# A load whose 16 queues read neighbouring rows: the order of the attention input in memory

## The chip, the cores and the metric

The kernel runs on one core of one Trainium2 chip. The core has a matrix engine (TensorE, in the profile PE for its matmuls and PEld for its weight loads), a vector engine (VectorE, DVE), a scalar engine (ScalarE, ACT), a general engine (GpSimd, POOL) and an engine that only issues transfers and waits (SyncE, SP). Each takes its instructions in order, and they meet through semaphores. Data lies in the chip's memory, in the on-chip memory SBUF with its 128 partitions, and in PSUM, where matmuls put their results. Transfers between memory and SBUF are done by 16 DMA engines, which serve the queues of SP, ACT and POOL; one issued transfer is shared out over them.

The metric is the device time of one execution in microseconds (us). Lower is better.

## The reference

Two stages. The first is a causal attention without softmax, in which older positions fade (a retention), for 8 sequences of 576 positions, 8 heads of 64 (rel is the position of the row less that of the column):

```python
scores = scale * np.matmul(q, k.transpose(0, 1, 3, 2))
gamma = 1.0 - 2.0 ** (-5.0 - np.arange(H, dtype=np.float32))
Dmat = np.where(rel >= 0, gamma[:, None, None] ** rel[None, :, :], 0.0)
ret = scores * Dmat[None, :, :, :]
return np.matmul(ret, v).astype(np.float32)
```

Its result, as 4608 tokens of 512 numbers, goes through a mixture of 8 experts, of which each token takes one or none (probs is the softmax of the logits, mask picks the tokens of expert e):

```python
do_compute = x @ w_skip > 0
xc = x[do_compute]
logits = xc @ w_gate
e_idx = np.argmax(logits, axis=1)
gate_w = probs[np.arange(len(xc)), e_idx]
for e in range(E):
    h = np.maximum(xc[mask] @ w1[e], 0.0)
    y[mask] = gate_w[mask, None] * (h @ w2[e])
out[do_compute] = xc + y
```

## The kernel before

**Attention.** The work is cut into 36 groups g of 128 tokens (two sequences of one pair, 64 positions each; nine groups in a row make a pair's 576 positions). A group has one tile u of 128 partitions by 4 slots by 512 numbers, 1 MB. The host has put queries, keys and values into the array qkv in the very order in which u wants them, so that a group is loaded by two transfers of 512 KB: load_half (L433 to L446) with s = 0 fills the slots 0 and 1 (queries and keys, for the scores), with s = 2 the slots 2 and 3 (values and keys, for the running state). Each transfer gives every partition one piece of 4 KB.

For each group, TensorE makes the scores (L476, 64x64 blocks), the update of the running state (L528), the values (L556), and turns the result back to rows (L578). VectorE multiplies by the decay tables (decay, L494; xt, L567). POOL scales the keys for the state (keys, L514, tile kn), out of the second half of u. ACT copies the state out of PSUM into the next group's u (L539) and the finished rows to xn (L580), which ACT's own queue stores to out (L581, 256 KB).

**The order of the loads.** TensorE's order is the program's order (L661). Five buffers of u exist (UBUFS), and loads run up to four groups ahead (UAHEAD). Before the loop, the loads of the groups 0 to 3 are issued one after the other (L455 to L460). Within the loop over g, the second half of group g+3 is issued after the first block of products of group g, on which it is made to wait (L697, last_product), and the first half of group g+4 after the values of group g-1, whose buffer it takes over (L707). All of them stand on SP's queue. From group 32 on nothing is left to load.

**Routing.** Beside the attention, the logits of finished tokens are made (logits_a, logits_b), and VectorE gives each token its place with its expert (route_a, route_b, slots). The expert with the most tokens among the first ones is begun early (choose_first, close_first); its first five weight pieces (load_w, L130, 512 KB each, also on SP's queue) are loaded among the last loads of u.

**Experts.** From about 182 us on, the eight experts follow in order of size. Each has eight pieces of weights, loaded by SP, split into a high and a low part by ACT (L139) and VectorE (L140), and multiplied three times for accuracy (L387). Tokens are gathered (L303) and put back (L836) by indirect transfers that POOL issues.

The load that the change touches is in L437 and L438, both sides 128 x 1024, and the host's side of it in L1037:

```python
u_t[g][:, s : s + 2].rearrange("p s c a i -> p (s c a i)"),
qkv[g, s // 2],
...
qkv = qkv.reshape(NT, 2, P, 2 * DM)
```

Row p of qkv[g, h] goes to partition p, and the 128 rows of a load lie one after the other in memory, 512 KB in one piece.

Of the kernel before, what the change touches and what calls it, by code (L numbers as in the profile page):

```python
# [22 lines left out]
NTOK, DM, NE, DF = B * S, H * D, 8, 1024  # L23
P = 128
NT = NTOK // P
# [2 lines left out]
NCC = DM // P  # L28
NFC = DF // P
NBLK = 3  # L30

CAPS = (368, 344, 332, 308, 304, 286, 278, 276)
CAP = CAPS[0]
# [23 lines left out]
def kernel(  # L57
# [36 lines left out]
    make_identity(nc, ident)  # L94
    iota = const.tile([P, NBLK * P], F16, tag="iota", name="iota")
    nc.gpsimd.iota(iota, pattern=[[1, NBLK * P]], base=0, channel_multiplier=0, allow_small_or_imprecise_dtypes=True)
    desc = const.tile([P, NE], F32, tag="desc", name="desc")
# [79 lines left out]
    def route_b(ps, first, late, pin, n, t0, ex, mb, cb):  # L177
        c0 = NE * NCMP * NBLK + t0 * NE
        pr = ps[:, c0 : c0 + n * NE]
# [44 lines left out]

    def slot_match(t, nb=NBLK):

        r = rs_t[t] = rt.tile([P, NBLK * P], BF16, tag="r", name=f"r_{t}", bufs=NR)
        nc.vector.tensor_scalar(r[:, : nb * P], iota[:, : nb * P], trank[:, t : t + 1], None, ALU.is_equal)  # L228

    def slot_add(ps, t, first, last, nb=NBLK):  # L230
        r = rs_t.pop(t)
        for k in range(nb):
            nc.tensor.matmul(
                ps[:, k * NE * NCMP : (k + 1) * NE * NCMP],
                r[:, k * P : (k + 1) * P],
                mc[:, t, :],
                start=first and k == 0,
                stop=last,
                skip_group_check=True,
            )  # L240
# [174 lines left out]
    with ExitStack() as actx:  # L415
# [17 lines left out]
        def load_half(g, s, after=None):  # L433
            if s == 0:
                u_t[g] = ap.tile([P, 4, 2, NPR, D], F32, tag="u", name=f"u_{g}", bufs=UBUFS)
            half = nc.sync.dma_start(
                u_t[g][:, s : s + 2].rearrange("p s c a i -> p (s c a i)"),  # L437
                qkv[g, s // 2],  # L438
            )
            if after is not None:  # L440
                tc.add_manual_dep(
                    half.ins,
                    after.name,
                    mybir.DependencyInfo(mybir.DependencyClass.Sync, mybir.DependencyReason.DATA),
                    reason="the second half begins behind a block of products",
                )  # L446

        def load_u(g):
            for s in (0, 2):
                load_half(g, s)  # L450
# [241 lines left out]
        for g in range(NT):  # L692
            ahead = g + 1 < NT
            for c in range(2):
                in_turn(state(g, c), *([scores(g + 1, c)] if ahead else []))
                if c == 0 and g and g + UAHEAD - 1 < NT:
                    load_half(g + UAHEAD - 1, 2, last_product())  # L697
# [8 lines left out]
            if g + UAHEAD < NT:  # L706
                load_half(g + UAHEAD, 0)  # L707
# [15 lines left out]
        g = NT  # L723
# [332 lines left out]
```

## Time and profile before

| | |
|---|---|
| median of 3 executions | 429.39 us |
| lowest and highest | 425.88 and 430.9 us |
| the profiled execution | 428.38 us |
| its span, first to last instruction | 426.6 us |
| mean granted TensorE clock | 0.971 |

The profile is of one execution. Its page gives the busy time of each engine, the span in 40 equal slices of 10.7 us (a digit is the busy share in tenths), the DMA queues, the chain of work that ended last, the costliest groups of instructions, and the DMA issues with their median time from issue to landing. An entry such as "L514 POOL ... kn<-u" is line 514 of the kernel, run on POOL, writing kn from u. In the lists of waits, "A <- B: us, times, longest" says how long A's engine stood idle until B released it. DMA share is the mean busy share of the 16 DMA engines, GB/s is what they moved. The queue q1 is SP's, q10 is ACT's, q0 POOL's.

### The profile page before, as it was taken

The page shows a single profiled execution, that of the slowest core. Times are in us where ns is not written, and L with a number is a line of the kernel's source. Part 1 is how long each engine was busy: PE and PEld are TensorE (multiplying, and loading weights), DVE is VectorE, ACT ScalarE, POOL GpSimd, SP SyncE. Part 2 cuts the span into 40 slices and gives each one's busy share as a digit, 9 for nine tenths or more (in the row PEclk, how much of TensorE's full clock was granted, in tenths as well). Part 3 has the DMA queues.
Part 4 walks back from the last instruction along what each step waited for, and adds up shares of the span by engine and source line. Part 5 has one row for each costly group of instructions (what it writes and reads, how often), then busy time and mean ns, then how long its engine had stood idle before and what let it go on. Part 6 is the DMA issues. An engine that isn't in the chain of part 4 may idle for free.

```text
span 426.6 us, 13158 instructions
## 1 busy us (share of the span) xinstructions
PE 383.3 (90%) x5482; PEld 349.2 (82%) x5484; DVE 272.9 (64%) x570; ACT 176.1 (41%) x296; POOL 148.9 (35%) x166
## 2 busy tenths in 40 slices
PE   7888777978796878999999999999999999999990
PEld 3676666866675756888999999999999999999980
DVE  2567694688579888948745565775665665656430
ACT  1334343354344446216444434444534445455210
POOL 5833643364365468060150043032042151400302
PEclk9989998999999889999999999999999999999996
DMA  8889997999989985363765456456456466652101
GB/s 305 310 290 339 311 325 249 328 334 305 311 296 349 338 315 163 103 220 117 267 201 181 148 171 211 149 189 205 163 177 221 154 222 204 199 157 89 52 2 53
DMA packets 29135, 93.05 MB, mean 218 GB/s; under 512 B 3960, under 2 KB 4344, under 8 KB 29072
## 3 DMA queue, kind: packets, MB, share of 16 engines
q1 hardware_dynamic: 19584, 71.31, 50.2%
q0 software_dynamic: 3728, 11.04, 7.6%
q10 hardware_dynamic: 5760, 9.82, 6.1%
q8 instruction: 44, 0.72, 0.7%
q14 instruction: 19, 0.16, 0.1%
HBM read 77.98 MB, written 14.55 MB: 217 GB/s over the span
## 4 chain that ended last, share of the span: by engine, by line
PE 44%; DMA 22%; issue 16%; DVE 10%; POOL 4%; ACT 1%; another core or an unknown queue 1%; POOLq 0%; ACTq 0%; SPq 0%
DMA out<-rs,sidx 15%; PE py L387 10%; PE ph L387 9%; PE pxt L556 7%; PE ps_s L528 5%; PE px L578 4%; DMA xg<-out,gidx 3%; PE psc L476 3%; DVE u L494 2%; POOL out L836 2%; DVE r L228 2%; PE pl L586 2%; DMA out<-xn 1%; DMA u<-qkv 1%; POOL xg L303 1%
## 5 line engine op out<-in xcount | busy, mean ns | idle before, releaser
L140 DVE TENSOR_TENSOR wlo_w<-w,whi_w 128x1024 fp32r<-128x1024 f32 x59 | 71.9, 1223 | 56.5 <-ACT whi_w L139 56.4
L514 POOL TENSOR_TENSOR kn<-u,tt_sb 64x512 f32<-64x512 f32 x64 | 67.5, 1054 | 74.3 <-DMA u<-qkv 51.5
L836 POOL DMA_INDIRECT out<-rs,sidx x24 | 32.7, 1363 | 151.0 <-DVE rs L835 147.7
L139 ACT CAST whi_w<-w 128x1024 fp32r<-128x1024 f32 x59 | 61.6, 1051 | 57.5 <-PE py L387 53.9
L387 PE MATMUL py<-hhi,whi_w 128*128 128x344 f32 (+6 forms) x224 | 70.2, 313 | 0.0
L494 DVE TENSOR_TENSOR u<-psc,dt_sb 64x512 f32<-64x512 f32 x72 | 49.6, 689 | 30.9 <-PE psc L476 15.7
L387 PE MATMUL ph<-xhi,whi_w 128*128 128x344 f32 (+6 forms) x224 | 68.9, 307 | 0.0
L387 PE MATMUL py<-hhi,wlo_w 128*128 128x344 f32 (+6 forms) x224 | 67.7, 302 | 0.0
L387 PE MATMUL ph<-xhi,wlo_w 128*128 128x344 f32 (+6 forms) x224 | 67.7, 302 | 0.0
L387 PE MATMUL ph<-xlo,whi_w 128*128 128x344 f32 (+6 forms) x224 | 67.7, 302 | 0.0
L387 PE MATMUL py<-hlo,whi_w 128*128 128x344 f32 (+6 forms) x224 | 67.5, 302 | 0.0
L539 ACT COPY u<-ps_s 64x512 f32<-64x512 f32 x64 | 37.1, 579 | 46.7 <-PE psc L476 18.3
L528 PEld LDWEIGHTS ps_s<-u,kn 64*64 64x64 f32 x1024 | 36.9, 142 | 21.5 <-issue 13.1
L476 PE MATMUL psc<-u 64*64 64x64 f32 x1152 | 47.8, 230 | 7.0 <-issue 6.9
L556 PE MATMUL pxt<-u 128*64 128x64 f32 x1152 | 46.0, 233 | 8.3 <-issue 8.3
L395 ACT ACTIVATE hhi<-ph 128x344 fp32r<-128x344 f32 (+8 forms) x61 | 26.0, 426 | 64.3 <-PE ph L387 62.1
L528 PE MATMUL ps_s<-u,kn 64*64 64x64 f32 x1024 | 43.2, 231 | 9.9 <-issue 8.4
L556 PEld LDWEIGHTS pxt<-u 128*64 128x64 f32 x1152 | 39.9, 145 | 13.6 <-issue 11.3
L476 PEld LDWEIGHTS psc<-u 64*64 64x64 f32 x1152 | 41.0, 141 | 8.1 <-issue 7.7
L387 PEld LDWEIGHTS ph<-xhi,whi_w 128*128 128x128 f32 x224 | 42.3, 189 | 0.1
L387 PEld LDWEIGHTS ph<-xlo,whi_w 128*128 128x128 f32 x224 | 42.3, 189 | 0.1
L387 PEld LDWEIGHTS py<-hlo,whi_w 128*128 128x128 f32 x224 | 42.3, 189 | 0.0
(178 smaller groups left out, 641.3 us busy)
## 6 DMA issues: line engine op xcount, KB each, us to landing
u<-qkv SPq DMA_DIRECT2D x72, 512.0 KB, 5.8
w<-w SPq DMA_DIRECT2D x64, 512.0 KB, 3.6
out<-xn ACTq DMA_DIRECT2D x36, 256.0 KB, 5.9
out<-rs,sidx POOLq DMA_INDIRECT x24
xg<-out,gidx POOLq DMA_INDIRECT x21
dt_sb<-dtab ACTq DMA_DIRECT2D x1, 128.0 KB
gt_sb<-dtab ACTq DMA_DIRECT2D x1, 128.0 KB
wg_sb<-wg ACTq DMA_DIRECT2D x1, 64.0 KB, 8.3
```

Source lines behind the costliest of these rows:

```text
L139: nc.scalar.copy(hi, t)
L140: nc.vector.tensor_tensor(lo, t, hi.bitcast(F32), ALU.subtract)
L387: nc.tensor.matmul(ps, x, y, start=first and n == 0, stop=last and n == 3 * len(terms) - 1)
L395: nc.scalar.activation(hi, ph, AF.Relu)
L476: nc.tensor.matmul(psc_t[g][halves[j], c, a, :], u[halves[j], 1 - j, c, a, :], u[halves[j], j, c, a, :], start=c == 0 and a == 0, stop=c = ...
L494: nc.vector.tensor_tensor(u_t[g][h, j], psc[halves[j]], tab, ALU.mult)
L514: nc.gpsimd.tensor_tensor(kn_t[g][h], u_t[g][h, 2 + j], tab, ALU.mult)
L528: nc.tensor.matmul(ps_s[halves[j], c, a, :], kn_t[g][h, c, a, :], u_t[g][h, 3 - j, c, a, :], start=n == 0 and c == 0 and a == 0, stop=c == ...
L539: nc.scalar.copy(u_t[g + 1][halves[j], 3 - j], ps_s[halves[j]])
L556: nc.tensor.matmul(pxt[halves[j], a, c * D : (c + 1) * D], u_t[g][:, 3 - j, c, a, :], u_t[g][:, j, c, a, :], start=c == 0 and a == 0, stop ...
L578: nc.tensor.transpose(px[:, c * P : (c + 1) * P], xt_t[b][:, c, o * P : (o + 1) * P], ident)
L836: put = nc.gpsimd.indirect_dma_start(out=out, out_offset=bass.IndirectOffsetOnAxis(ap=sidx[:n, k, e : e + 1], axis=0), in_=rs[:n], in_offs ...
```

## The change

The host writes the 128 rows of a load in another order, and the load reads them back in the old one. Row p goes to the same partition p as before, and no other line is touched.

```diff
+NQUEUE = 16
...
             half = nc.sync.dma_start(
                 u_t[g][:, s : s + 2].rearrange("p s c a i -> p (s c a i)"),
-                qkv[g, s // 2],
+                qkv[g, s // 2].rearrange("r e x -> e r x"),
             )
...
+    def by_row(x):
+
+        x = x.reshape(*x.shape[:2], NQUEUE, P // NQUEUE, x.shape[-1])
+        return np.ascontiguousarray(x.transpose(0, 1, 3, 2, 4))
+
...
-    qkv = qkv.reshape(NT, 2, P, 2 * DM)
+    qkv = by_row(qkv.reshape(NT, 2, P, 2 * DM))
```

With p = 8 e + r, e from 0 to 15 and r from 0 to 7, row p lay at place 8 e + r of the load's 512 KB; now it lies at place 16 r + e. The array qkv has the shape 36 x 2 x 8 x 16 x 1024 in place of 36 x 2 x 128 x 1024. The source of a load is described by 16 entries (4 KB apart) of 8 rows (64 KB apart) of 4 KB, in place of 128 rows of 4 KB. The tile's side of the load is described as before, by 128 partitions of 4 KB. In the words of the change, e is the queue and r the row of that queue.

## The prediction

> **What bounds the kernel now.** I read the page first (shares, slices, queues), then the busy time by stage, then the waits, and last the loads' own landing times.
>
> ```profile
> span 426.6 us, 13158 instructions
> ...
> PE 383.3 (90%) x5482; PEld 349.2 (82%) x5484; DVE 272.9 (64%) x570; ACT 176.1 (41%) x296; POOL 148.9 (35%) x166
> ...
> DMA  8889997999989985363765456456456466652101
> GB/s 305 310 290 339 311 325 249 328 334 305 311 296 349 338 315 163 103 220 117 267 201 181 148 171 211 149 189 205 163 177 221 154 222 204 199 157 89 52 2 53
> ...
> q1 hardware_dynamic: 19584, 71.31, 50.2%
> q0 software_dynamic: 3728, 11.04, 7.6%
> q10 hardware_dynamic: 5760, 9.82, 6.1%
> ...
> u<-qkv SPq DMA_DIRECT2D x72, 512.0 KB, 5.8
> w<-w SPq DMA_DIRECT2D x64, 512.0 KB, 3.6
> out<-xn ACTq DMA_DIRECT2D x36, 256.0 KB, 5.9
> ```
>
> The span has two halves. In the first 15 slices (about 160 us) the DMA engines are eight to nine tenths busy at some 310 GB/s; after that they are at half. Only the first half issues the loads that the change touches: 72 loads of 512 KB into u, 37.7 MB. The 64 loads of w have the same size and keep their layout; they are the control. The same queue, q1, carries both.
>
> Busy time by stage; the columns are named in the second line:
>
> ```profile
> core 0 of [0], span 426.6 us
> core 0: us, PE busy (x) PEld busy (x) DVE busy (x) ACT busy (x) POOL busy (x), PEclk, DMA share, GB/s
> 0.00:3.00 3.00, 1.72 (x5) 0.62 (x6) 0.29 (x3) 1.25 (x1) 2.34 (x24) 1.00 0.31 70
> 3.00:14.00 11.00, 8.94 (x136) 5.28 (x139) 4.07 (x6) 1.39 (x4) 6.34 (x11) 0.84 1.04 401
> 14.00:150.00 136.00, 111.92 (x3271) 93.17 (x3262) 100.31 (x225) 57.31 (x100) 65.93 (x68) 0.96 0.91 312
> 150.00:182.00 32.00, 28.18 (x436) 22.43 (x433) 28.14 (x101) 14.48 (x25) 15.92 (x22) 0.95 0.56 193
> 182.00:300.00 118.00, 117.07 (x775) 113.07 (x774) 73.47 (x139) 51.60 (x85) 30.93 (x25) 1.00 0.57 187
> 300.00:410.00 110.00, 110.00 (x846) 109.76 (x846) 63.27 (x93) 48.92 (x80) 24.55 (x18) 1.00 0.49 156
> ```
>
> From 182 us on PE is busy for 227 of 228 us: that half is PE's, and no load of u is in it. From 14 to 150 us PE is busy for 112 of 136 us and DMA's share is 0.91: two resources close together. The row from 3 to 14 us matters most. There loads of u run almost alone, all queues full, and move 401 GB/s.
>
> Who waits for whom, over the whole span:
>
> ```profile
> POOL kn L514 <- DMA u<-qkv: 51.5, 23, 8.3
> ...
> PEld ps_s L528 <- POOL kn L514: 7.4, 11, 1.0
> ...
> PE ps_s L528 <- POOL kn L514: 1.5, 2, 0.8
> ```
>
> and of the loads' issuing queue, SP:
>
> ```profile
> SPq L436 <- PE pxt L556: 57.3, 30, 4.9
> SPq L436 <- PE psc L476: 44.7, 31, 4.1
> ```
>
> SP waits 102 us for PE before it may issue loads (a buffer that comes free, or the product behind which a second half is put). POOL waits 51.5 us for loads, but of that only 7.4 us reach PE's weight loads and 1.5 us its matmuls. So today PE sets the pace of this stage, and the loads follow with a little room.
>
> The room itself comes from the last issues on SP:
>
> ```profile
> 137.64 0.35 SPq L130 DMA_DIRECT2D w<-w  x1
> 138.09 1.89 SPq L436 DMA_DIRECT2D u<-qkv  x2
> 140.18 0.54 SPq L130 DMA_DIRECT2D w<-w  x1
> 141.27 3.76 SPq L436 DMA_DIRECT2D u<-qkv  x2
> 145.24 0.34 SPq L130 DMA_DIRECT2D w<-w  x1
> 146.49 0.33 SPq L436 DMA_DIRECT2D u<-qkv  x1
> ```
>
> The last load of u is issued at 146.5 us and, with the 5.8 us to landing of the issue table, lands at about 152.3 us. The transfers before it, all at 401 GB/s: 72 loads of 524,288 B at 1.307 us are 94.1 us; some 30 stores of xn (the store of group g-2 goes out with group g, and the last load with group 32) at 0.654 us are 19.6 us; three loads of w are 3.9 us; some 2.5 us pass before the queues are full (the first 3 us moved 70 GB/s). Together 120.1 us, of which 26.0 us are not loads of u. So the loads have 152.3 - 120.1 = 32 us of room over the stage.
>
> **The change part by part.** *The host's reordering* (by_row) runs before the launch: 0 us. *The bytes* stay: 72 loads of 512 KB, each partition still gets 4 KB in one piece.
>
> *The issue.* The source has one dimension more (16 by 8 rows by 1024). An issue takes 0.33 us in the row at 146.49; whether the longer description costs more no row shows. Its ends: 0, and the 0.34 us more that would double it, 24 us for 72. SP has 102 us of waiting to cover that, so I take 0.
>
> *The order in memory.* For the read side the bounds come from rows of the present layout. The gain end: the best single microsecond of loads moves 430 GB/s.
>
> ```profile
> 13.00:14.00 1.00, 0.81 (x29) 0.55 (x31) 0.00 (x0) 0.38 (x1) 0.92 (x2) 1.00 1.10 430
> ```
>
> So a load could become 401/430 = 0.93 as long: 6.5 us less of transfer, and that in a stage with 32 us of room. Sixteen queues that together hold 401 GB/s for 11 us are not being held up by where their rows lie. I take 0 for it.
>
> *The order of the queues' work.* This is the step that I think decides. Before, both sides of the load count 128 rows, and whatever shares rows out to 16 queues can group them as it likes. After, the source counts 16 by 8 and the tile 128. If a queue takes one of the source's 16 entries, as the change's own numbering has it, queue e writes the partitions 8e to 8e+7. If the old grouping was another one, the queues' writes into the tile are now other than those that make 401 GB/s. The profile does not show which queue writes where, so the price is bounded: a factor of 0.93 at the one end (the 430 GB/s), and of 2 at the other, where two queues each time want the same way into the tile and take turns. Which value? The queues start together: one issue of 0.33 us feeds all 16, so partners meet row by row and stay in step, which is the upper end. The stores, a fifth of this stage's bytes (256 KB to 1 MB of loads per group), move between and push partners apart. I leave a quarter of the packets out of step: factor 1.75. In step, the 94.1 us become 164.7 us; with the other 26.0 us the last load lands at 190.7 us instead of 152.3 us. The stage is then DMA's, 38.4 us longer. Nothing covers that: the second half starts from the last group and is full of PE work. PE's work of the stage lies beside the transfers, as its 112 us are less.
>
> [...]
>
> *What is queued behind.* On SP the first expert's five loads of w stand among the last loads of u and move with them; they are needed only after the last group, which moves as far. POOL's kn waits for the second half of each u, and the copy into the next state waits for kn; these waits grow, and are the way in which the 38 us reach PE.
>
> **The sum.** The profiled execution took 428.4 us (426.6 us of span and 1.8 us around it), 1.0 us under the median of 429.4. 428.4 + 38.4 = 466.8, so 467 us. With the factor at 1.5 the last load lands at 167.2 us and the time is 443 us; at 2.0, 214.2 us and 490 us.
>
> **The rivals.** *No change that can be told, 428 us.* Up to a factor of (152.3 - 26.0) / 94.1 = 1.34 the loads stay within their room and PE sets the pace as now. This includes that the change does not do what it says: which rows a queue read before is nowhere in the profile, and if the 8 rows of a queue are the same as before, only the read side is changed, which the 401 GB/s show to be free. For it: the loads' present lead. Against: the tile's side is nearly full (0.91), so there is not much to lose before it counts.
>
> *Faster, 420 us.* The mechanism: rows that are asked for at the same time lie next to each other, memory answers sooner, kn starts sooner, and PE's waits behind kn go. The price is at most those waits, 7.4 + 1.5 = 8.9 us, so 419.5 us; it decides from about half of them on. For it: in the stage a unit of DMA share moves 312/0.91 = 343 GB/s, against 401/1.04 = 386 at the start, so a packet takes 1.12 times as long as in loads alone. Against: stores, and not the layout, are what the stage has and the start has not. [...]
>
> **How the numbers follow.** About 1%, 4.3 us, is what a measurement of this kernel can tell from no change (its three runs spread from 425.9 to 430.9). Slower by the queues' new split: 0.64. Within 1%: 0.23. Faster: 0.13. The forecast is the first case, 467 us, and its own range is 440 to 490 us (factors 1.5 to 2.0). As the second case is needed for 8 in 10, the range goes down to 425 us; left out are the faster case and what little lies over a factor of 2.
>
> **What would show it.** The landing times of loads alone, of u to 20 us and of w from 180 us on:
>
> ```profile
> L436 SPq DMA_DIRECT2D u<-qkv x13: 327/328/757, 0.8 to 19.4; - x13
> ...
> DMA to landing us min/median/max: 4.1/5.3/7.7
> ```
>
> ```profile
> L130 SPq DMA_DIRECT2D w<-w x55: 332/333/337, 180.0 to 385.8; - x55
> ...
> DMA to landing us min/median/max: 3.4/3.5/5.9
> ```
>
> If I am right, u's landing grows by half or more while w's stays at 3.5 us; the window from 3 to 14 us moves about 401/1.75 = 229 GB/s at a share near 1; the last load of u is issued near 185 us; POOL's waits for u go well over 51.5 us while SP's for PE shrink; q1's share rises to (214 + 71) / 465 = 61% (50.2% of 426.6 us is 214 us); and the stage from the last group to the end keeps its length. I am wrong if the window from 3 to 14 us still moves 400 GB/s: then the queues' split costs nothing. If it moves less but over 300 GB/s, the factor stays under 1.34 and the time within 1%. An issue on SP of over 0.6 us would show the longer description.

## The result and the profile after

The changed kernel is slower: 457.94 us (453.89 to 462.28, 4 executions) against 429.58 us (425.88 to 430.9, 4 executions). The ratio is 1.064, with a 95% interval from 1.054 to 1.075. Here and below a time is the median of all executions, while a ratio leaves out the slow ones (over 1.5% above the fastest of the same kernel), so it is not exactly the quotient of two medians. The profiled execution took 457.51 us, its span 455.8 us.

From the page of the changed kernel: span, slices, queues and issues.

```profile
span 455.8 us, 13158 instructions
...
DMA  8999999999999999644376645645656566463101
GB/s 190 238 260 267 285 268 263 268 329 259 272 249 258 283 273 298 225 152 139 117 271 203 209 132 163 203 138 191 210 152 228 182 207 215 146 202 119 49 1 50
...
q1 hardware_dynamic: 19584, 71.31, 54.9%
...
u<-qkv SPq DMA_DIRECT2D x72, 512.0 KB, 7.4
w<-w SPq DMA_DIRECT2D x64, 512.0 KB, 4.1
out<-xn ACTq DMA_DIRECT2D x36, 256.0 KB, 5.7
```

The packets and bytes of q1 are the same to the last one. But the DMA engines are now nine tenths busy in the first 16 slices and move some 265 GB/s there, where they moved some 310. The load of u lands after 7.4 us, not 5.8.

Busy time by stage, changed kernel (span of the stage, then PE, PEld, DVE, ACT and POOL busy with their instructions, granted clock, DMA share, GB/s):

```profile
3.00:14.00 11.00, 6.34 (x105) 3.96 (x103) 2.84 (x4) 0.20 (x2) 2.42 (x6) 0.92 1.05 236
14.00:150.00 136.00, 105.39 (x2777) 86.87 (x2773) 80.94 (x174) 48.44 (x85) 56.88 (x59) 0.87 0.99 269
```

This is the plainest sign. From 3 to 14 us the DMA engines of both kernels do almost nothing but load u, with full queues, at a share of 1.04 and 1.05; the one moves 401 GB/s, the other 236. A load takes 401/236 = 1.70 times as long. From 14 to 150 us the share is 0.99 (it was 0.91): nothing is left of the room, and DMA sets the pace. PE got through 2777 matmuls in this window, not 3271. Its granted clock fell as well, from 0.96 to 0.87, and a matmul took 105.39/2777 = 38 ns of busy time, not 34. No run separates what this does to the time; that the DMA share is full speaks for the loads as the limit.

Waits of the changed kernel, among them those that answer to the waits shown before:

```profile
POOL kn L515 <- DMA u<-qkv: 88.0, 26, 8.6
...
ACT u L540 <- POOL kn L515: 27.1, 6, 13.6
...
PEld ps_s L529 <- POOL kn L515: 6.8, 7, 3.1
...
PE ps_s L529 <- POOL kn L515: 3.0, 1, 3.0
```

of the queue that issues the loads:

```profile
SPq L437 <- PE pxt L557: 58.8, 31, 5.7
SPq L437 <- PE psc L477: 57.1, 26, 5.2
```

the wait of ACT for POOL in the kernel before:

```profile
ACT u L539 <- POOL kn L514: 17.2, 8, 9.0
```

and the last issues on SP, changed kernel:

```profile
171.63 0.43 SPq L131 DMA_DIRECT2D w<-w  x1
172.45 0.55 SPq L437 DMA_DIRECT2D u<-qkv  x1
```

POOL waits 88.0 us for loads (51.5 before), and ACT's copy of the state waits 27.1 us for POOL (17.2 before). PE's own waits for kn hardly change: 6.8 us of PEld and 3.0 us of PE, where it was 7.4 and 1.5. These sums are loose signs. In the five runs below that are as fast as the kernel before (entries of 4 or 2 rows), POOL waits 55.3 to 68.7 us for loads, and in two of them ACT waits 20.2 and 27.1 us for POOL. The last load of u is issued at 172.4 us; it was 146.5 us. From there to the end of the span it is 283.4 us, and was 280.1 us. So of the 29.2 us that the span grew, 26.0 us lie before the last load of u, and 3.2 us behind it.

### The profile page after: what moved, and what is told of

It is laid out like the page before. It is cut to its first block, busy times and chain, and to the rows that moved or that the text cites. A ratio compares the mean times of both kernels' runs of the same rounds, so it can differ in the third digit from the quotient of the medians.

```text
span 455.8 us, 13158 instructions
## 1 busy us (share of the span) xinstructions
PE 393.8 (86%) x5482; PEld 358.6 (79%) x5484; DVE 267.6 (59%) x570; ACT 176.0 (39%) x296; POOL 145.8 (32%) x166
## 3 DMA queue, kind: packets, MB, share of 16 engines
q1 hardware_dynamic: 19584, 71.31, 54.9%
## 4 chain that ended last, share of the span: by engine, by line
PE 63%; DMA 17%; issue 12%; DVE 3%; POOL 1%; ACT 1%; SPq 0%; ACTq 0%; POOLq 0%
PE py L388 16%; PE ph L388 15%; DMA out<-rs,sidx 11%; PE pxt L557 9%; PE ps_s L529 6%; PE px L579 5%; DMA u<-qkv 5%; PE psc L477 3%; PE pl L587 2%; PE pt L800 2%; PE yn L834 1%; DMA xg<-out,gidx 1%; PE pn L602 1%; DMA xg<-out,gl 1%; PE ph L405 1%
## 5 line engine op out<-in xcount | busy, mean ns | idle before, releaser
L515 POOL TENSOR_TENSOR kn<-u,tt_sb 64x512 f32<-64x512 f32 x64 | 66.5, 1038 | 99.8 <-DMA u<-qkv 88.0
L495 DVE TENSOR_TENSOR u<-psc,dt_sb 64x512 f32<-64x512 f32 x72 | 49.6, 689 | 45.2 <-PE psc L477 27.1
L529 PE MATMUL ps_s<-u,kn 64*64 64x64 f32 x1024 | 46.1, 240 | 17.8 <-issue 12.7
L529 PEld LDWEIGHTS ps_s<-u,kn 64*64 64x64 f32 x1024 | 39.6, 150 | 27.7 <-issue 17.9
L540 ACT COPY u<-ps_s 64x512 f32<-64x512 f32 x64 | 37.1, 580 | 58.7 <-POOL kn L515 27.1
L477 PE MATMUL psc<-u 64*64 64x64 f32 x1152 | 50.9, 238 | 10.3 <-issue 8.5
L557 PE MATMUL pxt<-u 128*64 128x64 f32 x1152 | 50.2, 248 | 9.0 <-issue 9.0
L557 PEld LDWEIGHTS pxt<-u 128*64 128x64 f32 x1152 | 44.0, 159 | 16.5 <-issue 13.2
L477 PEld LDWEIGHTS psc<-u 64*64 64x64 f32 x1152 | 43.7, 149 | 12.0 <-issue 9.6
```

The source lines that it names most:

```text
L477: nc.tensor.matmul(psc_t[g][halves[j], c, a, :], u[halves[j], 1 - j, c, a, :], u[halves[j], j, c, a, :], start=c == 0 and a == 0, stop=c = ...
L495: nc.vector.tensor_tensor(u_t[g][h, j], psc[halves[j]], tab, ALU.mult)
L515: nc.gpsimd.tensor_tensor(kn_t[g][h], u_t[g][h, 2 + j], tab, ALU.mult)
L529: nc.tensor.matmul(ps_s[halves[j], c, a, :], kn_t[g][h, c, a, :], u_t[g][h, 3 - j, c, a, :], start=n == 0 and c == 0 and a == 0, stop=c == ...
L540: nc.scalar.copy(u_t[g + 1][halves[j], 3 - j], ps_s[halves[j]])
L557: nc.tensor.matmul(pxt[halves[j], a, c * D : (c + 1) * D], u_t[g][:, 3 - j, c, a, :], u_t[g][:, j, c, a, :], start=c == 0 and a == 0, stop ...
```

## The experiments

The theory, called W: the description of the source decides which partitions a queue writes, and with 16 entries of 8 rows pairs of queues get in each other's way on the tile's side. The rivals: R, neighbouring rows asked for at once slow the memory down; D, the third dimension of the description slows the queues' work by itself.

**Order and description apart.** The first run keeps the old order in memory under the new description:

```diff
-                qkv[g, s // 2].rearrange("r e x -> e r x"),
+                qkv[g, s // 2][:, : P // NQUEUE, :],
...
-        return np.ascontiguousarray(x.transpose(0, 1, 3, 2, 4))
+        return np.concatenate([x, x[:, :, :, :1]], axis=3)
```

> The rows of a load lie in the old order (8 e + r), but the source is described as 16 entries of 8 rows; one unused row after every eight keeps the description from falling together into 128 rows. Theory W (write side: the description decides which partitions a queue writes, and pairs of queues get in each other's way at the tile): as the changed kernel, 236 GB/s from 3 to 14 us and about 458 us. Rival R (read side: neighbouring rows asked for at once slow the memory down): as the kernel before, about 401 GB/s and 429 us. Rival D (the third dimension of the description makes the queues' work itself slower): as W, 236 GB/s, 458 us.

The second keeps the neighbours' order and three dimensions, but makes 32 entries of 4 rows:

```diff
-NQUEUE = 16
+NQUEUE = 32
```

> The rows lie in neighbours' order as in the change, but by 32 entries of 4 rows (row r of entry e at 32 r + e), and the source is described as 32 by 4 by 1024. W: two entries of 4 rows for each queue can be shared out as before the change, so 400 GB/s from 3 to 14 us and 425 to 432 us. If the 32 entries are shared out two neighbours to a queue, W gives the 458 us of the change again. R: neighbouring rows as in the change, so 236 GB/s and 458 us. D: three dimensions as in the change, 236 GB/s and 458 us. An issue on SP takes 0.54 us under all three. [...]

The window from 3 to 14 us, in the first run and then in the second:

```profile
3.00:14.00 11.00, 6.82 (x106) 4.29 (x106) 3.18 (x5) 0.20 (x2) 2.42 (x6) 0.78 1.03 242
```

```profile
3.00:14.00 11.00, 7.21 (x109) 4.17 (x108) 4.09 (x6) 1.36 (x4) 6.23 (x11) 0.86 1.02 389
```

Old order, 16 by 8: 242 GB/s, 455.28 us, ratio 1.053 (1.046 to 1.060). Neighbours' order, 32 by 4: 389 GB/s, 429.46 us, ratio 0.993 (0.988 to 0.997). The description decides, and the order makes no difference that can be told (236 and 242 GB/s, and the intervals of 1.064 and 1.053 overlap): R falls by both runs. D falls by the second, which has three dimensions and the longer issue too:

```profile
L437 SPq DMA_DIRECT2D u<-qkv x72: 534/535/987, 0.8 to 147.5; - x72
```

0.535 us for an issue, against 0.328 before, and the time of before: SP's waiting covers it.

**Where the queues meet.** If W is right, what matters is which partitions are written at the same time. Two runs load the first four groups in pieces, all with the same description (8 by 8 in the first pieces); later groups are as in the change:

```diff
+        def load_part(g, s, e0, e1):
+            n = P // NQUEUE
...
+            nc.sync.dma_start(
+                u_t[g][e0 * n : e1 * n, s : s + 2].rearrange("p s c a i -> p (s c a i)"),
+                qkv[g, s // 2][:, e0:e1].rearrange("r e x -> e r x"),
+            )
...
+        for part in ((0, 8), (8, 16)):
+            for g in range(UAHEAD):
+                for s in (0, 2):
+                    load_part(g, s, *part)
```

and ((4, 12), (0, 4), (12, 16)) in the other run. The first pieces are thus the partitions 0 to 63 of all eight loads, or 32 to 95.

> The loads of the first four groups are cut: first the partitions 0 to 63 of all eight loads (8 entries of 8 rows, so at most 8 queues), then 64 to 127; later groups as in the change. Read from 3 to 12 us, as GB/s for a whole DMA share: the loads alone made 401/1.04 = 386 before the change, 236/1.05 = 225 in the change. W with partners 32 partitions apart: queue e writes 8 e to 8 e + 7, so 0 to 31 and 32 to 63 meet; 225 to 260, some 120 GB/s. If fewer queues alone end the trouble: 386, some 195 GB/s. The total time is that of the change, about 458 us, under both.

> As the run that begins at partition 0, but the first pieces are the partitions 32 to 95, then 0 to 31 and 96 to 127 (4 entries of 8 rows each). Eight queues, the same description, the same rows for each queue; only the partitions differ. W with partners 32 partitions apart within one half of the 128: 32 to 63 and 64 to 95 have no partners among them, so 386 GB/s for a whole share, some 195 GB/s from 3 to 12 us. If a straight share of 8 rows to a queue is slow wherever it lies: as from 0, 225 to 260 and some 120 GB/s. [...]

From 5 to 13 us, when only first pieces are under way, from 0 and then from 32:

```profile
5.00:13.00 8.00, 1.84 (x6) 0.49 (x4) 0.00 (x0) 0.00 (x0) 1.75 (x3) 0.81 0.55 149
```

```profile
5.00:13.00 8.00, 1.07 (x4) 0.25 (x2) 0.00 (x0) 0.00 (x0) 0.00 (x0) 0.74 0.53 212
```

The shares of 0.55 and 0.53, half the 1.05 of the change, fit loads that about half the DMA engines carry. From 32 the pieces move 212 GB/s, 400 for a whole share, as fast as the kernel before. From 0 they move 149 GB/s, 271 for a whole share, a little over the 225 to 260 expected. (The expectations named 3 to 12 us; there it is 212/0.58 = 366 from 32 and 153/0.58 = 264 from 0.) Only the partitions differ, and with them the rows read, whose order was seen not to matter. So the partitions that are written at the same time set the rate here: 271 GB/s for a whole share into 0 to 63, 400 into 32 to 95. That fits W as both expectations have it, with partners 32 partitions apart, a distance that the author assumed and that these two runs alone test. Which two queues meet, no trace shows. The whole times, one execution each (465.36 and 470.6 us), say little, since the later groups are the change's and the pieces that come second have 8 or 4 entries.

**Longer turns.** With 8 entries of 16 rows:

```diff
-NQUEUE = 16
+NQUEUE = 8
```

> Neighbours' order with 8 entries of 16 rows, described as 8 by 16 by 1024. If only 8 queues can then carry a load, 8 x 401/16 = 200 GB/s from 3 to 14 us are the most. W with partners in each other's way as in the change: 200/1.7 = 118 GB/s, the loads take 320 us, about 620 us in all. If queues that write 16 neighbouring partitions do not meet, 200 GB/s and 37.7 MB / 200 GB/s + 26 us = 215 us to the last landing, about 491 us in all. [...]

490.94 us (one execution). Two windows of it:

```profile
5.00:20.00 15.00, 6.08 (x102) 4.44 (x101) 3.42 (x6) 0.00 (x0) 2.33 (x3) 0.58 0.54 147
24.00:44.00 20.00, 15.31 (x395) 13.20 (x390) 9.63 (x18) 4.65 (x8) 7.85 (x8) 0.74 0.55 222
```

Neither expectation holds for the whole run, though its time is the second one's (about 491 us). At first the rate is that of the pieces from 0: 147/0.54 = 272 GB/s for a whole share. From about 24 us on it is that of the pieces from 32: 222/0.55 = 404. Why this run gets free, while the change still moves only 269/0.99 = 272 for a whole share from 14 to 150 us, no run shows.

**The other loads.** u as before the change, and w in the new form:

```diff
-w[bass.ds(regs[e], 1), f].rearrange("o p c -> (o p) c")
+w[bass.ds(regs[e], 1), f].rearrange("o r e c -> (o e) r c")
...
-    w = np.ascontiguousarray(np.concatenate([w1, moe_w2.reshape(NE, NFC, P, DM)], axis=3))
+    w = by_row(np.concatenate([w1, moe_w2.reshape(NE, NFC, P, DM)], axis=3))
```

> u is loaded as before the change, and the 64 loads of w take the new form (16 by 8, neighbouring rows) instead. W, R and D alike: a load of w that stands alone takes 1.31 us x 0.7 = 0.9 us longer, so its median landing in the experts' half goes from 3.5 to 4.4 us, and the first 14 us stay at 401 GB/s. As PE is busy for 227 of 228 us from 182 us on, nothing of that reaches the end: 427 to 433 us. If the loads' lateness counted wherever it falls, 64 x 0.9 = 58 us would be added: 487 us.

Loads of w from 210 us on:

```profile
L131 SPq DMA_DIRECT2D w<-w x50: 539/540/582, 210.5 to 390.8; - x50
...
DMA to landing us min/median/max: 4.7/5.0/5.2
```

434.09 us, ratio 1.006 (1.002 to 1.010), 1 us over the range expected. A load of w lands 1.5 us later than before, not 0.9; some 0.2 us of that is the issue, 0.54 against 0.33 us. The other 1.3 us might be read as a factor of 2 on its transfer of 1.31 us, but the packets do not bear that out:

```profile
q1 hardware_dynamic: 19584, 71.31, 57.3%
```

57.3% of 431.6 us is 247 us, 33 more than the 214 before, or some 0.5 us for each of 64 loads: a factor of about 1.4. Where the rest of the later landing comes from is open. Of 64 x 1.5 = 96 us at most some 3 reach the end, because PE has work there whether or not the loads land early, 169.88 of 170 us:

```profile
210.00:380.00 170.00, 169.88 (x1205) 168.19 (x1203) 105.82 (x170) 78.68 (x125) 43.82 (x33) 1.00 0.76 192
```

Whether the 3 us are the loads' at all is not shown: further down, a kernel with a w that is left alone comes out at 1.006 too, and at 1.001 the other time.

**Half the loads.** Only the second halves in the new form:

```diff
-                qkv[g, s // 2].rearrange("r e x -> e r x"),
+                (qkv[g, 1].rearrange("r e x -> e r x") if s else qkv[g, 0].rearrange("r e x -> (r e) x")),
```

> Only the second halves (slots 2 and 3, 36 loads) take the new order and the description 16 by 8; the first halves are loaded as before. W, with the 1.70 that the start of the changed kernel showed: 36 x 1.307 + 36 x 1.307 x 1.70 + 26 = 153 us to the last landing, as long as the 152 us that PE's pace gave the stage before. So the room is just used up: 429 to 437 us, far less than half of the 28 us. If each slow load cost its own time, half of the loads would cost half: 444 us.

446.83 us against 430.58 us beside it, ratio 1.040 (1.033 to 1.048). The expectation missed, and with it the idea of a room of 32 us. From 14 to 150 us, and the packets of SP's queue:

```profile
14.00:150.00 136.00, 104.40 (x2956) 85.39 (x2954) 90.50 (x189) 51.27 (x90) 60.66 (x63) 0.94 0.99 286
...
q1 hardware_dynamic: 19584, 71.31, 54.0%
```

DMA is already full, at 286 GB/s. The packets took 54.0% of 442.4 us, 239 us, 25 more than the 214 before. A room of 32 us would have swallowed them; instead the kernel lost 16.3 us. So the room was some 9 us. Half the loads brought 25 of the 36 us that all of them bring (54.9% of 455.8 us is 250). Why more than half is open: the first halves may be disturbed when some queues are still in a second half. That was not tried.

**Does the order help under 32 by 4?** The ratio of 0.993 above asks for it. The old order under 32 by 4, twice; the neighbours' order again; and 64 entries of 2 rows. The first is the second run above with the old-order edit of the first; the last sets NQUEUE to 64.

> The old order in memory (4 e + r, one unused row after every four), described as 32 by 4. Beside the run with neighbours' order and the same description it tells what the order alone does. If neighbouring rows help by the 0.7% that the other run showed against the kernel before: 1.000 here. If the longer issue or the spare share makes that 0.7%: 0.993 here too. W in both cases: 400 GB/s from 3 to 14 us and 426 to 433 us.

> Neighbours' order, 32 by 4, a second time and beside the old order with the same description. If neighbouring rows help: 0.993 again, below 1 with its interval. If the first 0.993 was chance: 0.997 to 1.003, the interval with 1 in it.

> Old order, 32 by 4, a second time: 0.997 to 1.003 as at first, under both readings.

> Neighbours' order by 64 entries of 2 rows, described as 64 by 2. W: four entries of 2 rows still make up what a queue had before the change, so 400 GB/s from 3 to 14 us. If neighbouring rows help: 0.99 to 0.995. If they don't: 0.997 to 1.003. If 64 entries are shared out four neighbours to a queue: 236 GB/s and 1.064 as the change.

| order, description | us | ratio (95%) |
|---|---|---|
| neighbours, 32 by 4 | 429.46 | 0.993 (0.988 to 0.997) |
| neighbours, 32 by 4, again | 432.09 | 1.002 (0.997 to 1.007) |
| neighbours, 64 by 2 | 431.34 | 1.001 (0.997 to 1.005) |
| old, 32 by 4 | 431.15 | 1.001 (0.996 to 1.005) |
| old, 32 by 4, again | 432.72 | 1.006 (1.002 to 1.010) |

All five load at 389 to 401 GB/s from 3 to 14 us. The same kernel gave 0.993 and 1.002, and another 1.001 and 1.006, so a difference of half a per cent is not to be told here, and no gain of the neighbours' order is shown. The quotients of the medians all lie between 0.997 and 1.003. No version tried is shown to beat the kernel before.

## Why the prediction was right, and where its sizes were not

*The place and the mechanism* held. The change costs almost alone in the attention stage (26.0 of 29.2 us before the last load of u), by way of the loads' transfer. The window from 3 to 14 us moved 236 GB/s, where the forecast had 229 and named 400 as the sign of an error. The loads up to 20 us, which landed after 5.3 us, land after 9.9:

```profile
L437 SPq DMA_DIRECT2D u<-qkv x10: 536/588/715, 0.8 to 18.9; - x10
...
DMA to landing us min/median/max: 7.9/9.9/14.3
```

*The way into PE* is not shown. The forecast named kn and the copy of the state behind it. POOL's wait for loads rose to 88.0 us, beyond the 68.7 us that a run as fast as before can show, but such a run can show ACT's 27.1 us too, and PE's own waits for kn grew by 0.9 us in all. The longest waits of PE in this stage, 12.7, 9.0 and 8.5 us, are put down to "issue", that is, to nothing that the profile shows.

*The read side at 0* held, with an argument that covered only half of it. The forecast bounded what the new order could gain, and had no place for a loss (R above). Under either description, both orders load at rates within 3% of each other from 3 to 14 us (236 and 242 GB/s with 16 by 8; 389 and 393 against 397 and 396 with 32 by 4).

*The issue at 0* held. It takes 0.21 us more, which the row of before could not show, and SP covers it: with this issue and entries of 4 rows the time is that of before.

*The split of the queues' work* was the step on which all hung, and it held as far as rates can tell: the description sets the rate under either order (236 and 242 GB/s with 16 by 8, 389 and 397 with 32 by 4), and the choice of partitions sets it under one description (271 and 400 GB/s for a whole share). That two queues each time want the same way into the tile and take turns was the author's assumption; no run shows which queue writes where.

*The size* was off, in two terms that partly cancel. The first is the factor of 1.75 for the whole stage. At the start it was 1.70, but the sign that the forecast had named for the whole, q1's share, came out at 54.9% and not 61%: the packets took 36 us more, not 71. By the forecast's own 94.1 us that is a factor of 1.38. The forecast's quarter of packets out of step was too small a part, or stepping out gains more than it thought; no run tells these apart. The second is the room of 32 us, counted at the 401 GB/s of loads alone. Where loads run beside stores, a full share moved 312/0.91 = 343 GB/s even before the change. By the share left over, 0.09 of 136 us, the room was 12 us. The runs say some 10: with all loads changed, 36 us of packets moved the last load by 26.0 us, and with half of them, 25 us cost 16.3 us. So the rival "no change" was given more than it had. That the time came as near as 457.9 to 467 is luck: with the 36 us measured, the forecast's own room would have given about 432 us.

A sum by shares, made afterwards from the measured rates, comes close. From 3 to 14 us (401 - 236) x 11 us = 1.8 MB stay behind, 6.7 us at the later 272 GB/s for a full share. The 42.4 MB of the window from 14 to 150 us take 42.4/272 = 156 us in place of 136. Together 26.7 us, near the 26.0 us by which the last load moved.

*What was foreseen and did not come so:* SP's waits for PE were to shrink from 102 us, and grew to 58.8 + 57.1 = 116 us. A load waits for a buffer that PE must free, also when PE itself is late for want of loads, so this wait does not tell which of the two sets the pace. The last load of u was issued at 172.4 us, not near 185. And w's landing was to stay at 3.5 us; its median from 210 us on is 4.0 us (3.3 to 7.1), with the layout of w untouched. It is 3.5 us (3.4 to 7.4) with 32 entries of 4 rows, where u loads as fast as before. It does not reach the end, and its cause is open.

## What to carry to other kernels

The dimensions in which a load is described were not only a matter of addresses here: the same 512 KB moved at 389 to 401 GB/s when described as 128 rows, 32 entries of 4 rows or 64 of 2, and at 236 to 242 as 16 entries of 8. The author's reading, which fits these rates, is that the outermost dimension decides how the rows are shared out over the queues, and so which partitions are written at the same time. With 8 entries the DMA share was 0.53 to 0.59 while loads ran almost alone, with 16 to 64 it was 1.01 to 1.05. No trace shows the sharing itself, and the reading leaves open why 8 entries of 16 rows moved 272 GB/s for a whole share at first and 404 from about 24 us on. Before anything else, look at the rate of the loads alone. At 401 GB/s, near the best window's 430, a new order of the addresses had nothing to win here. To judge how much slower a transfer may become, take the rate for a full DMA share in the stage itself, and not that of loads alone: the room was 10 to 12 us here, not 32.

## What was not expected of the hardware

Loads described as 16 by 8 did not lose a fixed factor. In full queues they lost a factor of 1.70 at the start, and all 72 together only 1.38 by their packets' time. A load of w by itself lost about 0.5 us on 1.31 us by its packets, and yet landed 1.5 us later. Loads described as 8 by 16 ran at the slow rate for some 20 us and from then on at the full one (272 GB/s for a whole share, then 404). With one dimension more in the description an issue on SP took 0.535 to 0.537 us with 16, 32 or 64 entries and 0.596 us with 8, instead of 0.328 us.
